# Row statistics ahead of the mixing stage, and a filter's wrap-around term added by accumulating DMAs, in a gated convolution and token-mixing kernel

## The chip, the cores and the metric

The kernel runs on one core of one Trainium2 chip. The metric is the device time of one execution in microseconds (us), the lower the better. The profile's "span" runs from the first to the last recorded instruction and is about 1.8 us shorter than the reported time (203.6 against 205.44 in the profiled run of the kernel before). All times given as positions ("at 50.2") count from the start of the span.

The engines are named as in the profile: PE is TensorE (matmul), DVE is VectorE, ACT is ScalarE, POOL is GpSimd. SP issues most DMAs. "Granted clock" is the share of TensorE's full clock that its throttle let through.

## The reference

For x = q of shape [2048, 640], in bf16:

```python
g = sigmoid((x * gate_w).sum(-1))            # one gate per row
# a: a short convolution of k (4 taps), times v, then a long causal convolution, times q
kv = short_conv(k, shift_k) * v
a  = q * (irfft(rfft(pad(kv, 4096)) * rfft(pad(ssm_k, 4096)))[:2048] + kv * ssm_D)
# b: LayerNorm over a row, then an MLP that mixes along the 2048 rows
h  = layernorm(x)                            # row mean and variance
u  = gelu(einsum("sd,sf->df", h, w1) + b1)   # F = 1536
b  = (einsum("df,fs->ds", u, w2) + b2).T
out = g * a + (1 - g) * b
```

The two halves a and b share only x, g and the last line. Matmuls of b can fill the time in which TensorE waits for data of a.

## The kernel before

The stages, with the names that the profile's tiles have:

- Filter spectra: TensorE turns `ssm` into `wT` and multiplies it with DFT matrices `FTB`; ScalarE copies the results from PSUM into `C[0]` and `C[1]`; VectorE's "mixing" finishes the spectra with additions and subtractions. The index h = 0 or 1 says which half of the 2048 positions is meant.
- kv: k is reordered (`kp<-kn`) and transposed by DMA into `KT`; 80 matmuls for each half (`KF,KT`) do the short convolution into `ksh`; VectorE multiplies with v (`vkv` for the first half, `kv` for the second).
- kv spectra: 64 matmuls per half (`vkv,FTB`, `kv,FTB`), evacuated by ScalarE into `C[2]` and `C[3]`, mixed by VectorE.
- MLP: 384 matmuls `X,ring` (first layer; X is x after normalising, `ring` holds the layer's weights as they are loaded), GELU into `GT`, 384 matmuls `GT,W` (second layer, with its weights `W`).
- Output: VectorE multiplies spectra (`tm<-C,C` and so on), TensorE transforms back with the matrices `GTB` (`C,GTB` and `SS,GTB`), VectorE multiplies by q and adds b.

While it is being built, the kernel puts all operations into a list scheduler, which has assumed durations, priorities (`prio`, the lower goes first) and the dependencies it finds from overlapping memory.

Memory is nearly full, so buffers share places. `GT`, the first layer's result, is 12 blocks of 1280 bytes per partition, and its place serves others earlier:

```python
        ksh = [alloc(f"ksh{i}", [128, 4, D], BF16, at=base_of(GT) + 5120 * (1 + i)) for i in range(2)]
        rows = alloc("rows", [20, 4, 512], BF16, at=base_of(GT))
        kp = [alloc("kp0", ..., at=base_of(ring[1]) + 10240), alloc("kp1", [128, NG, 128], BF16, at=base_of(GT))]
```

So the first four blocks of GT are also `kp1` (the reordered k of blocks 1 and 3), and the other eight are `ksh`. The filter loop, v1mix, the gate and the first layer:

```python
        for h in range(2):
            # ... transposes of the filter
            for p in PORD:
                fwd(srcW(h), h, p, C[h], p, 1.0 / 1024.0, "W")      # forward DFT and evacuation
            for kt in range(2):
                for p in range(4):
                    ln_tile(2 * h + kt, p)          # bn_stats, bn_aggr on VectorE
                ln_apply(2 * h + kt)                # rstd on GpSimd, X=(X-mean)*rstd on VectorE
            if h == 0:
                for g0 in (0, 10):
                    tt("POOL", KF[:, g0:g0 + 10, :, :], ...)         # taps times a mask, on GpSimd
                for hk in range(2):
                    k_turn(hk)
                mixing(C[0], SS, 0, fine=True)
            else:
                mixing(C[1], C[0], 0)
        # ...
        def v1mix(Wh, Ws, Vh, Vs):                  # V += or -= W, real and imaginary parts exchanged
            def ap(h, s, o, st):
                return V(h, s * SL + o, [[SL, 2], [st, 2], [1, D]])
            tt("DVE", ap(Vh, Vs, 0, 3 * D), ap(Vh, Vs, 0, 3 * D), ap(Wh, Ws, 2 * D, -D), ALU.add)
            tt("DVE", ap(Vh, Vs, D, D), ap(Vh, Vs, D, D), ap(Wh, Ws, 3 * D, -3 * D), ALU.subtract)

        v1mix(C[0], 2, C[1], 2)
        v1mix(SS, 0, C[0], 0)
        # ... kv and its spectra ...
        for ft in range(FT):
            vt = _VT("mlp")
            for hk in range(4):
                # 8 matmuls X,ring per hk; prio 10**6 + 4*ft + hk: they fill what is left
                mms(vt, items, prio=10 ** 6 + 4 * ft + hk, name="m1")
            act(GT[:, ft, :]..., two, ACT.Gelu_apprx_tanh, ..., vt=vt, prio=0, name="gelu")
        # ...
        tt("POOL", gth[:, :], vtmp[:, :], rstd[:, :], ALU.mult)      # the gate, 128x16 elements
        # ... seven more small operations, tanh on ScalarE among them
```

## Time and profile before

| | before |
|---|---|
| time, median of 3 runs | 205.58 us (205.1 to 205.8) |
| span of the profiled run, mean granted clock | 203.6 us, 0.975 |
| TensorE busy, VectorE busy | 180.8 us (89%), 182.0 us (89%) |

Five lines of the profile's page for the kernel before: the busy time of each engine, three rows of the view in 40 slices (each digit the busy share, or the granted clock, in tenths; a slice is 5.1 us), and the engines' shares of the chain of work that ended last.

```profile
PE 180.8 (89%) x1403; PEld 131.5 (65%) x1403; DVE 182.0 (89%) x193; ACT 116.1 (57%) x183; POOL 48.8 (24%) x33
...
PE   0769989951599999999999799999999999999993
...
DVE  8896999989989999989999999999949957997462
...
PEclk9999999996589999999999999999999999999999
...
PE 67%; DVE 17%; POOL 6%; DMA 3%; issue 2%; ACT 2%; SPq 0%; DVEq 0%; POOLq 0%
```

TensorE and VectorE are equally busy. From the ninth to the eleventh slice (41 to 56) TensorE falls to 5, 1 and 5 tenths, and its clock is low from the tenth to the twelfth. Where is the time lost? The timeline of TensorE has the answer. Its columns are the start, the duration, the engine, line, operation, output and inputs with shapes, the count, and in brackets the idle time before and what ended it.

```profile
39.06 4.33 PE L293 MATMUL pp<-KF,KT 128*128 128x128 bf16 x80
50.17 0.69 PE L293 MATMUL pp<-vkv,FTB 128*128 128x320 bf16 x2 [6.78 <-DVE vkv L617]
52.95 10.00 PE L293 MATMUL pp<-vkv,FTB 128*128 128x320 bf16 x54 [2.09 <-DVE vkv L617]
...
113.13 17.55 PE L293 MATMUL pp<-X,ring 128*128 128x320 bf16 x128 [1.46 <-ACT GT L655]
...
186.12 4.56 PE L293 MATMUL pp<-C,GTB 128*128 128x320 bf16 x32
...
194.91 5.60 PE L293 MATMUL pp<-GT,W 128*128 128x320 bf16 x40
```

After the short convolution (to 43.4) TensorE has nothing until 50.17, does two matmuls and waits again until 52.95; both waits end with VectorE's `vkv`. Then 54 matmuls take 10.00 us, 0.185 each, while later ones of the same shape take 0.136 to 0.137 (17.55/128). A smaller pause of 1.46 stands at 111.7. At the end 40 second-layer matmuls (5.60) come after the last inverse transform.

The same stretch by windows: length, then busy time and count of PE, PEld (weight loads), DVE, ACT and POOL, then the granted clock, the DMA share and GB/s.

```profile
43.40:50.10 6.70, 0.00 (x0) 0.00 (x0) 6.70 (x12) 1.39 (x2) 0.00 (x0) 0.80 0.94 391
50.10:52.90 2.80, 0.69 (x2) 0.14 (x2) 2.80 (x4) 0.00 (x0) 0.00 (x0) 0.50 0.38 78
```

VectorE is busy in all of this time, 6.70 of 6.70 us: it is not slow to start but has other work ahead of `vkv`. The mean clock is 0.80 in the first window and 0.50 in the second. The Trainium skill ("TensorE: Matmul & The Clock Gate", section "Part 1: The HAM clock gate") says that TensorE drops to half its clock after an idle window of about 3.4 us and regains it after a busy one; this trace agrees for the 6.78 us pause: in finer windows the granted clock is 1.00 up to 47.4, which is 4.0 us into the pause, then 0.50, and 1.00 again from 58.0.

VectorE's timeline in the kernel before, same columns:

```profile
48.54 1.48 DVE L617 TENSOR_TENSOR vkv<-ksh,vkv 128x2560 bf16<-128x2560 bf16 x1
...
51.41 1.48 DVE L617 TENSOR_TENSOR vkv<-ksh,vkv 128x2560 bf16<-128x2560 bf16 x1
...
64.11 2.88 DVE L617 TENSOR_TENSOR C<-C,C 128x2560 bf16<-128x2560 bf16 x2
66.91 2.88 DVE L617 TENSOR_TENSOR C<-C,SS 128x2560 bf16<-128x2560 bf16 x2
...
121.57 2.83 DVE L617 TENSOR_TENSOR tm<-C,C 128x5120 bf16<-128x5120 bf16 x1
...
181.52 2.89 DVE L617 TENSOR_TENSOR C<-SS 128x2560 bf16<-128x2560 bf16 x2
```

The two `vkv` products come at 48.54 and 51.41. The four additions of v1mix are the `C<-C,C x2` and `C<-C,SS x2` at 64.1 to 69.8, 5.6 us. The last two lines are landmarks: the first product of the output stage at 121.57, and the step at 181.52 whose first half (done at about 183.0) the last inverse half needs.

And GpSimd's two slowest gate operations:

```profile
74.20 14.03 POOL L627 TENSOR_SCALAR gpre<-mv,gws 128x16 f32<-128x16 f32 x1 [16.99 <-ACT junk L655]
105.53 5.67 POOL L617 TENSOR_TENSOR gth<-gth,gacc 128x16 f32<-128x16 f32 x1 [17.31 <-ACT junk L655]
```

They have 16 elements per partition and take 14.03 and 5.67 us (`gpre` and `gth` are intermediate values of the gate; `junk` is the discarded output of ScalarE's row sums). They do not compute for that long: the next addition of the same size took 0.77. From 74.20 to 88.02 VectorE went through eleven instructions with hardly a gap and then paused for 0.59; the first one ended in that pause.

### The profile page before, as it was taken

The page shows a single profiled execution, that of the slowest core. Times are in us where ns is not written, and L with a number is a line of the kernel's source. Part 1 is how long each engine was busy: PE and PEld are TensorE (multiplying, and loading weights), DVE is VectorE, ACT ScalarE, POOL GpSimd, SP SyncE. Part 2 cuts the span into 40 slices and gives each one's busy share as a digit, 9 for nine tenths or more (in the row PEclk, how much of TensorE's full clock was granted, in tenths as well). Part 3 has the DMA queues.
Part 4 walks back from the last instruction along what each step waited for, and adds up shares of the span by engine and source line. Part 5 has one row for each costly group of instructions (what it writes and reads, how often), then busy time and mean ns, then how long its engine had stood idle before and what let it go on. Part 6 is the DMA issues. An engine that isn't in the chain of part 4 may idle for free.

```text
span 203.6 us, 3356 instructions
## 1 busy us (share of the span) xinstructions
PE 180.8 (89%) x1403; PEld 131.5 (65%) x1403; DVE 182.0 (89%) x193; ACT 116.1 (57%) x183; POOL 48.8 (24%) x33
## 2 busy tenths in 40 slices
PE   0769989951599999999999799999999999999993
PEld 0446555640357877777776577788888867887672
DVE  8896999989989999989999999999949957997462
ACT  4798999970388989899640312123223164433752
POOL 2539700020520049930029600521000000000000
PEclk9999999996589999999999999999999999999999
DMA  5999999997898000007502700499999903110122
GB/s 165 338 405 278 344 335 197 198 400 322 159 229 283 5 0 0 0 3 234 178 3 63 246 0 3 106 236 315 236 306 404 351 11 129 69 64 0 64 93 104
DMA packets 35631, 35.00 MB, mean 172 GB/s; under 512 B 15515, under 2 KB 32544, under 8 KB 35616
## 3 DMA queue, kind: packets, MB, share of 16 engines
q1 hardware_dynamic: 34464, 32.15, 51.0%
q0 software_dynamic: 1088, 2.62, 6.8%
q8 instruction: 11, 0.18, 0.4%
q14 instruction: 4, 0.03, 0.0%
q10 hardware_dynamic: 64, 0.01, 0.0%
HBM read 25.87 MB, written 2.62 MB: 140 GB/s over the span
## 4 chain that ended last, share of the span: by engine, by line
PE 67%; DVE 17%; POOL 6%; DMA 3%; issue 2%; ACT 2%; SPq 0%; DVEq 0%; POOLq 0%
PE pp L293 67%; DVE X L628 4%; DVE stats L842 4%; DMA X<-in_A_q_dram 3%; DVE C L617 3%; POOL gth L617 3%; DVE SS L617 3%; POOL KF L617 2%; DVE kp L724 1%; DVE vkv L617 1%; POOL rstd L617 1%; ACT junk L655 1%; DVE mv L844 1%; SPq L267 0%; POOL gpre L617 0%
## 5 line engine op out<-in xcount | busy, mean ns | idle before, releaser
L293 PE MATMUL pp<-X,ring 128*128 128x320 bf16 x384 | 53.6, 299 | 1.5 <-ACT GT L655 1.5
L293 PE MATMUL pp<-GT,W 128*128 128x320 bf16 x384 | 52.9, 299 | 0.0
L617 DVE TENSOR_TENSOR C<-C 128x2560 bf16<-128x2560 bf16 (+1 forms) x28 | 48.7, 1766 | 3.2 <-DMA C<-C 2.6
L293 PEld LDWEIGHTS pp<-GT,W 128*128 128x128 bf16 x384 | 43.5, 114 | 8.8 <-ACT O L655 0.2
L293 PEld LDWEIGHTS pp<-X,ring 128*128 128x128 bf16 x384 | 37.4, 98 | 16.2 <-issue 1.8
L655 ACT ACTIVATE C<-pp 128x640 bf16<-128x640 f32 x64 | 40.0, 794 | 12.6 <-PE pp L293 12.1
L655 ACT ACTIVATE O<-pp,c,omg 128x640 bf16<-128x640 f32 (+1 forms) x17 | 14.5, 852 | 34.5 <-PE pp L293 34.5
L617 DVE TENSOR_TENSOR tm<-C,C 128x2560 bf16<-128x2560 bf16 (+1 forms) x12 | 22.7, 1926 | 0.0
L293 PE MATMUL pp<-wT,FTB 128*128 128x320 bf16 x128 | 20.1, 313 | 0.5 <-ACT wT L655 0.4
L655 ACT ACTIVATE GT<-pp,cc 128x640 bf16<-128x640 f32 x12 | 9.4, 789 | 18.6 <-PE pp L293 18.6
L293 PE MATMUL pp<-vkv,FTB 128*128 128x320 bf16 x64 | 11.9, 351 | 8.9 <-DVE vkv L617 8.9
L627 POOL TENSOR_SCALAR gpre<-mv,gws 128x16 f32<-128x16 f32 x1 | 14.0, 14028 | 17.0 <-ACT junk L655 17.0
L617 DVE TENSOR_TENSOR C<-tm 128x1280 bf16<-128x1280 bf16 (+1 forms) x16 | 17.9, 1153 | 0.2
L655 ACT ACTIVATE cgb<-pp,gg 128x640 bf16<-128x640 f32 x16 | 12.7, 793 | 8.0 <-PE pp L293 8.0
L293 PEld LDWEIGHTS pp<-wT,FTB 128*128 128x128 bf16 x128 | 10.8, 101 | 9.5 <-ACT C L655 4.4
L293 PEld LDWEIGHTS pp<-vkv,FTB 128*128 128x128 bf16 x64 | 6.6, 111 | 13.9 <-issue 6.9
L293 PE MATMUL pp<-ident,ssm 128*128 128x128 bf16 x80 | 8.8, 267 | 6.7 <-DMA ssm<-in_A_ssm_k_dram 5.4
L842 DVE BATCH_NORM_STATS2 stats<-X 128x6 f32<-128x320 bf16 x32 | 13.6, 463 | 0.5 <-DMA X<-in_A_q_dram 0.5
L293 PE MATMUL pp<-C,GTB 128*128 128x320 bf16 x96 | 13.7, 299 | 0.0
L628 DVE TENSOR_SCALAR X<-X,mv,rstd 128x640 bf16<-128x640 bf16 x16 | 9.6, 667 | 3.6 <-POOL rstd L617 3.6
L293 PEld LDWEIGHTS pp<-ident,ssm 128*128 128x128 bf16 x80 | 6.3, 128 | 9.2 <-DMA ssm<-in_A_ssm_k_dram 5.4
L655 ACT ACTIVATE junk<-gq 128x640 bf16<-128x640 bf16 x16 | 11.8, 736 | 0.5
(62 smaller groups left out, 195.2 us busy)
## 6 DMA issues: line engine op xcount, KB each, us to landing
ring<-in_B_w_dram SPq DMA_DIRECT2D x12, 512.0 KB, 6.0
W<-in_B_w_dram SPq DMA_DIRECT2D x8, 768.0 KB, 9.4
ssm<-in_A_ssm_k_dram SPq DMA_DIRECT2D x4, 640.0 KB, 9.0
X<-in_A_q_dram SPq DMA_DIRECT2D x4, 640.0 KB, 9.1
kn<-in_A_k_dram SPq DMA_DIRECT2D x4, 640.0 KB, 7.3
C<-C POOLq DMA_DIRECT2D x4, 640.0 KB, 11.7
out_dram<-O SPq DMA_DIRECT2D x7, 320.0 KB, 2.3
vkv<-in_A_v_dram SPq DMA_DIRECT2D x2, 640.0 KB, 5.2
```

The lines of the kernel that those rows point to most:

```text
L293: ins = self.nc.tensor.matmul(ps_ap, lhsT=lhsT, rhs=rhs, start=start, stop=stop, skip_group_check=True)
L617: return SC.add(eng, d, lambda s: T.op(eng, lambda e: e.tensor_tensor(o, a, b, op), [a, b], [o]), [a, b], [o], prio=prio, name="tt")
L627: return e.tensor_scalar(o, a, s1, None, op0=op0)
L628: return e.tensor_scalar(o, a, s1, s2, op0=op0, op1=op1)
L655: return T.op("ACT", lambda e: e.activation(o, src, func, **kw), rr + [src], ww)
L724: SC.add("DVE", 0.85, lambda s: T.op("DVE", lambda e: e.tensor_copy(ov, iv), [i[:, :, :]], [o[:, :, :]]), [i[:, :, :]], [o[:, :, :]], prio ...
L842: SC.add("DVE", 0.46, (lambda o, i: lambda s: T.op("DVE", lambda e: e.bn_stats(o, i), [i], [o]))(o, i), [i], [o])
L844: SC.add("DVE", 0.2, (lambda o, i: lambda s: T.op("DVE", lambda e: e.bn_aggr(o, i), [i], [o]))(o, i), [i], [o])
```

## The change

The intent: finish the row statistics and x early, so that first-layer matmuls can run while kv is not there; take 5.6 us of additions from VectorE, the co-bound engine, by letting DMAs accumulate; and free the gate chain from GpSimd. The accumulating DMAs used here add, so the signs must be in the stored spectra already: some ScalarE evacuations get a negative scale, mixing of the later half and the cross products get other signs, and GTB's imaginary part is negated on ScalarE ahead of the second inverse half. There is also a one-line move of `kp1`, from GT's place to GTB's.

```diff
-        kp = [alloc("kp0", ...), alloc("kp1", [128, NG, 128], BF16, at=base_of(GT))]
+        kp = [alloc("kp0", ...), alloc("kp1", [128, NG, 128], BF16, at=base_of(GTB))]
 ...
-            for kt in range(2):
-                for p in range(4):
-                    ln_tile(2 * h + kt, p)
-                ln_apply(2 * h + kt)
+                fwd(..., (lambda c, k2: k2 == 1) if h == 0 else (lambda c, k2: c == 1))   # negative scales
             if h == 0:
+                for hk in range(4):
+                    for p in range(4):
+                        ln_tile(hk, p)
+                    ln_apply(hk)
 ...
-                mixing(C[1], C[0], 0)
+                mixing(C[1], C[0], 0, conj=True)
 ...
         def v1mix(Wh, Ws, Vh, Vs):
-            tt("DVE", ap(Vh, Vs, 0, 3 * D), ap(Vh, Vs, 0, 3 * D), ap(Wh, Ws, 2 * D, -D), ALU.add)
-            tt("DVE", ap(Vh, Vs, D, D), ap(Vh, Vs, D, D), ap(Wh, Ws, 3 * D, -3 * D), ALU.subtract)
+            for i in range(2):
+                dma(V(Vh, (Vs + i) * SL, [[1280, 2], [1, 1280]]), V(Wh, (Ws + i) * SL + 1280, [[-1280, 2], [1, 1280]]),
+                    128 * 5120 * 2, stream="POOL", prio=0, accum=True)
 ...
-        tt("POOL", gth[:, :], vtmp[:, :], rstd[:, :], ALU.mult)      # and six more of the gate
+        tt("DVE", gth[:, :], vtmp[:, :], rstd[:, :], ALU.mult, mode=1, prio=0)
 ...
-                tt("DVE", comp(V1[g], i, 0), comp(T1, 0, 0), comp(T1, 0, 1), ALU.subtract)
-                tt("DVE", comp(V1[g], i, 1), comp(T1, 1, 0), comp(T1, 1, 1), ALU.add)
+                tt("DVE", comp(V1[g], i, 0), comp(T1, 0, 0), comp(T1, 0, 1), ALU.add)
+                tt("DVE", comp(V1[g], i, 1), comp(T1, 1, 1), comp(T1, 1, 0), ALU.subtract)
 ...
         inverse(1, Z1)
+        for p in (0, 2, 1, 3):
+            gk = GTB[:, p, :, :, 1, :]
+            act(gk, gk, ACT.Copy, scale=-1.0, name="neg")
```

More of the change, by code (lines that the diff above doesn't have):

```diff
@@ L592, in _build @@
         kn = [alloc(f"kn{i}", [128, 4, D], BF16, at=base_of(ring[1]) + 5120 * i) for i in range(2)]
-        kp = [alloc("kp0", [128, NG, 128], BF16, at=base_of(ring[1]) + 10240), alloc("kp1", [128, NG, 128], BF16, at=base_of(GT))]
+        kp = [alloc("kp0", [128, NG, 128], BF16, at=base_of(ring[1]) + 10240), alloc("kp1", [128, NG, 128], BF16, at=base_of(GTB))]
         pint = alloc("pint", [128, 4, 2, 2, 256], I32, at=base_of(ring[1]))
@@ L806, in transp, with fwd @@
             act(wT[:, hk, p, :], full, ACT.Copy, vt=vt, name="wT")
-        def fwd(src, h, p, dst, slot, scale, name):
+        def fwd(src, h, p, dst, slot, scale, name, neg=lambda c, k2: False):
             for k2 in range(2):
@@ L817, in fwd, with mixing @@
                     o = dst[:, slot, 2 * c + k2, :].rearrange("p (a b) -> p a b", a=2)
-                    kw = {} if scale is None else {"scale": scale}
+                    sc = -scale if neg(c, k2) else scale
+                    kw = {} if sc == 1.0 else {"scale": sc}
                     act(o, two, ACT.Copy, vt=vt, name=name + "e", **kw)
-        def mixing(R, Th, Ts, fine=False):
+        def mixing(R, Th, Ts, fine=False, conj=False):
             def sl(h, s, n=1):
@@ L833, in mixing @@
             oB = V(Th, Ts * SL, [[3 * 1280, 2], [1, 1280]])
+            if conj:
+                oA, oB = oB, oA
             tt("DVE", oA, pr(R, 0), pr(R, 1, True), ALU.add)
@@ L859, in _build @@
             for p in PORD:
-                fwd(srcW(h), h, p, C[h], p, 1.0 / 1024.0, "W")
-            for kt in range(2):
-                for p in range(4):
-                    ln_tile(2 * h + kt, p)
-                ln_apply(2 * h + kt)
+                fwd(srcW(h), h, p, C[h], p, 1.0 / 1024.0, "W", (lambda c, k2: k2 == 1) if h == 0 else (lambda c, k2: c == 1))
             if h == 0:
+                for hk in range(4):
+                    for p in range(4):
+                        ln_tile(hk, p)
+                    ln_apply(hk)
                 for g0 in (0, 10):
@@ L886, in v1mix @@
         def v1mix(Wh, Ws, Vh, Vs):
-            def ap(h, s, o, st):
-                return V(h, s * SL + o, [[SL, 2], [st, 2], [1, D]])
-            tt("DVE", ap(Vh, Vs, 0, 3 * D), ap(Vh, Vs, 0, 3 * D), ap(Wh, Ws, 2 * D, -D), ALU.add)
-            tt("DVE", ap(Vh, Vs, D, D), ap(Vh, Vs, D, D), ap(Wh, Ws, 3 * D, -3 * D), ALU.subtract)
+            for i in range(2):
+                dma(V(Vh, (Vs + i) * SL, [[1280, 2], [1, 1280]]), V(Wh, (Ws + i) * SL + 1280, [[-1280, 2], [1, 1280]]),
+                    128 * 5120 * 2, stream="POOL", prio=0, accum=True)
         v1mix(C[0], 2, C[1], 2)
@@ L922, in _build @@
         for p in PORD:
-            fwd(lambda kt, p, ci: vkv0[:, kt, p, 320 * ci:320 * ci + 320], 0, p, C[2], p, None, "A")
+            fwd(lambda kt, p, ci: vkv0[:, kt, p, 320 * ci:320 * ci + 320], 0, p, C[2], p, 1.0, "A")
         mixing(C[2], C[1], 0)
@@ L927, in _build @@
         for p in PORD:
-            fwd(lambda kt, p, ci: kv1[:, kt, p, 320 * ci:320 * ci + 320], 1, p, C[3], p, None, "A")
+            fwd(lambda kt, p, ci: kv1[:, kt, p, 320 * ci:320 * ci + 320], 1, p, C[3], p, 1.0, "A", lambda c, k2: k2 == 1)
         mixing(C[3], C[2], 0)
@@ L955, in _build @@
                         act(junk[:, :], gb[:, b, :], ACT.Copy, acc=gacc[:, t:t + 1], name="gsum")
-        tt("POOL", gth[:, :], vtmp[:, :], rstd[:, :], ALU.mult)
-        tt("POOL", gth[:, :], gth[:, :], gacc[:, :], ALU.mult)
-        ts("POOL", gpre[:, :], mv[:, :, 0], gws[:, 0:1], None, ALU.mult)
-        tt("POOL", gpre[:, :], gpre[:, :], gth[:, :], ALU.add)
-        act(gth[:, :], gpre[:, :], ACT.Tanh, scale=0.5)
-        ts("POOL", gg[:, :], gth[:, :], 0.5, 0.5, ALU.mult, ALU.add)
-        ts("POOL", omg[:, :], gth[:, :], -0.5, 0.5, ALU.mult, ALU.add)
-        tt("POOL", c2[:, :].rearrange("p (a b) -> p a b", a=4), omg[:, :].rearrange("p (a b) -> p a b", a=4), b2f, ALU.mult)
+        tt("DVE", gth[:, :], vtmp[:, :], rstd[:, :], ALU.mult, mode=1, prio=0)
+        tt("DVE", gth[:, :], gth[:, :], gacc[:, :], ALU.mult, mode=1, prio=0)
+        ts("DVE", gpre[:, :], mv[:, :, 0], gws[:, 0:1], None, ALU.mult, mode=1, prio=0)
+        tt("DVE", gpre[:, :], gpre[:, :], gth[:, :], ALU.add, mode=1, prio=0)
+        act(gth[:, :], gpre[:, :], ACT.Tanh, scale=0.5, prio=0)
+        ts("DVE", gg[:, :], gth[:, :], 0.5, 0.5, ALU.mult, ALU.add, mode=1, prio=0)
+        ts("DVE", omg[:, :], gth[:, :], -0.5, 0.5, ALU.mult, ALU.add, mode=1, prio=0)
+        tt("DVE", c2[:, :].rearrange("p (a b) -> p a b", a=4), omg[:, :].rearrange("p (a b) -> p a b", a=4), b2f, ALU.mult, mode=1, prio=0)
         def w2_load(hk):
```

## The prediction

> **What bounds it now.** Times are microseconds from the span's start (span 203.6; the reported time is about 2 longer). The page gives TensorE 89%, VectorE 89%; the chain of waits is 67% TensorE. TensorE has three losses (timeline, windows): a hole from 43.4 to 52.95 (only two matmuls), because kv reaches it late through VectorE's queue; a granted clock of 0.50 just after, so that 54 matmuls took 10.0 instead of 7.4 at the later pitch of 0.136; and a 1.5 hole at 111.7, where ScalarE sat 6.7 behind the gate chain on GpSimd. VectorE hardly idles before 146: a second, nearly equal bound.
>
> **What changes.** (1) All row statistics come before mixing, so x is normalised by about 40 instead of 58.4. The order view then puts 80 first-layer matmuls (10.9 at 0.136) ahead of the kv spectra, into the hole. (2) v1mix's four additions leave VectorE (5.6, at 64.1 to 69.7) for four accumulating DMAs. The existing four took 11.7 to land (median); the new ones are issued near 62 and needed from 87, so no wait. (3) The gate chain leaves GpSimd, where one 128x16 operation took 14.0 and one 5.7 while VectorE ran without a break. That agrees with the Trainium skill, "SBUF — State Buffer", section "SBUF: two separate sides": the port pair the two share is locked for a whole instruction. On VectorE it is eight operations of 0.1 to 0.2. (4) Four sign flips of GTB on ScalarE, estimated 0.6 each, are hidden.
>
> **Critical path, by hand in the new order with the trace's durations.** VectorE: normalising still loses 4 behind GpSimd's KF product (one instruction took 4.07 at 20.3); x blocks come at about 25, 28, 33 and 40, and TensorE waits about 2 to 4 for them. kv is ready at 55 to 56 (now 52.9). TensorE starts its spectra near 57 without having stopped and ends them near 70 (now 65), 104 first-layer matmuls further on. VectorE runs dry at about 64 and waits to 70 for these spectra: this swallows the 5.6 that v1mix freed. At the first inverse products (now 121.6) it stands at 121 to 125, the upper end because the tanh queues behind a GELU on ScalarE. TensorE, some 12 ahead, does 320 instead of 240 second-layer matmuls before the first inverse transform (near 163, as now) and has none left at the end. The last inverse half waits for VectorE: it starts near 184 (now 186.1), takes 8.7, then a tail of 4 to 4.5 (now 3.1, after 5.6 of second-layer work). Span about 197.
>
> **Prediction: 199.0 us, 194.0 to 203.5.** Faster by over 2%: 0.75; within 2%: 0.20; slower: 0.05. Much of TensorE's recovered 12 is not cashed, because VectorE becomes the bound.
>
> **Right if** the profile shows: no TensorE hole over 3 between 43 and 53, clock 1.0 there; VectorE busy about 177 instead of 182, with a new idle stretch of 4 to 7 near 64 to 70 ended by ScalarE's evacuation of kv spectra; the hole at 111.7 gone; TensorE waiting 1 to 6 for VectorE before the last inverse half; inverse matmuls last.
>
> **Wrong if** GpSimd's small column copy for the second half of k loses the race for the shared ports and waits for a VectorE pause (TensorE would stall several microseconds near 57); if the new DMAs land over 20 late and stop the cross products; or if the tanh holds VectorE longer than 2. Faster than 194 if the wait near 64 to 70 is much shorter.

## More of the kernel before

No engine has a fixed program order in the source.

```python
# in _Sched.add: an evacuation's dependencies are put on the first matmul of its group
            else:
                for d in deps:
                    if d.vt is not vt:
                        if d not in vt.first.deps:
                            vt.first.deps.add(d)
```

## The result

| | before | after |
|---|---|---|
| time, median of 4 runs | 205.69 us (205.1 to 205.93) | 198.8 us (197.93 to 199.71) |
| ratio of fast runs, 95% interval | | 0.967 (0.961 to 0.973) |
| span of the profiled run, granted clock | 203.6 us, 0.975 | 196.1 us, 0.996 |
| TensorE, VectorE busy | 180.8, 182.0 us | 177.4, 177.0 us |

Ratios here and below are the mean time of one kernel's fast runs over the mean time of the kernel before's fast runs in the same rounds on the same chip, so they are not quite the ratio of the medians quoted. Executions over 1.5% slower than the fastest of the same kernel are left out of the means. The kernel is faster by 3.3%.

The same five lines of the page, for the changed kernel (a slice is now 4.9 us):

```profile
PE 177.4 (90%) x1403; PEld 131.4 (67%) x1403; DVE 177.0 (90%) x196; ACT 118.5 (60%) x187; POOL 28.6 (15%) x30
...
PE   0759987999999999999999999999999979997890
...
DVE  7996998799999179999999879999999599989994
...
PEclk9999999999999999999999999999999999999998
...
PE 67%; DVE 16%; DMA 9%; ACT 3%; POOL 2%; issue 2%; SPq 0%; DVEq 0%
```

The low slices of TensorE and the dip of its clock are gone. VectorE has a new low slice, the fourteenth (64 to 69). The share of DMA in the chain rose from 3% to 9%, because the loads of k now stand in it (5%, by the page's list by line).

TensorE's timeline, after:

```profile
25.09 0.44 PE L293 MATMUL pp<-X,ring 128*128 128x320 bf16 x2 [0.32 <-DVE X L628]
...
31.49 1.42 PE L293 MATMUL pp<-X,ring 128*128 128x320 bf16 x8 [0.76 <-DVE X L628]
...
39.37 1.43 PE L293 MATMUL pp<-X,ring 128*128 128x320 bf16 x8 [0.49 <-DVE X L628]
...
46.06 4.33 PE L293 MATMUL pp<-KF,KT 128*128 128x128 bf16 x80
50.23 4.51 PE L293 MATMUL pp<-X,ring 128*128 128x320 bf16 x32
...
55.37 0.43 PE L293 MATMUL pp<-vkv,FTB 128*128 128x320 bf16 x2
...
182.28 4.63 PE L293 MATMUL pp<-C,GTB 128*128 128x320 bf16 x32 [2.22 <-DVE C L617]
186.80 4.51 PE L293 MATMUL pp<-SS,GTB 128*128 128x320 bf16 x32
```

First-layer matmuls (`X,ring`) now run from 23.8 on. Eighty of them precede the first `vkv,FTB` at 55.37, 32 of them from 50.23 on, in the old hole. Three short waits for x remain, 0.32, 0.76 and 0.49, and one of 2.22 before the last inverse half. Nothing but that half's 64 matmuls is left at the end.

VectorE's timeline, after:

```profile
20.33 4.35 DVE L724 COPY kp<-kn 128x2560 bf16<-128x2560 bf16 x1
...
53.14 2.89 DVE L617 TENSOR_TENSOR vkv<-ksh,vkv 128x2560 bf16<-128x2560 bf16 x2
55.94 8.68 DVE L617 TENSOR_TENSOR C<-C 128x5120 bf16<-128x5120 bf16 x5
69.90 2.83 DVE L617 TENSOR_TENSOR C<-C 128x5120 bf16<-128x5120 bf16 x1 [5.28 <-ACT C L655]
...
114.54 0.17 DVE L628 TENSOR_SCALAR gg<-gth 128x16 f32<-128x16 f32 x1 [1.14 <-ACT gth L655]
...
123.71 2.83 DVE L617 TENSOR_TENSOR tm<-C,C 128x5120 bf16<-128x5120 bf16 x1
...
180.74 2.89 DVE L617 TENSOR_TENSOR C<-SS 128x2560 bf16<-128x2560 bf16 x2
```

The copy `kp<-kn` at 20.33 took 4.35 us where its siblings took 0.8: GpSimd's product KF ran from 19.97 to 24.00. `vkv` is ready at 54.5 and 56.0, 3 to 4.5 us later than before, but TensorE no longer stands still for it. v1mix is gone from VectorE, and in its place stands a wait of 5.28 for ScalarE's evacuation of the kv spectra. The first product of the output stage starts at 123.71, 2.1 us later than before, and the landmark step at 180.74, only 0.8 earlier.

GpSimd's timeline, after: the issues of the four new DMAs.

```profile
60.60 2.64 POOL L262 DMA_DIRECT2D C<-C  x2 [21.72 <-DVE C L617]
64.92 2.43 POOL L262 DMA_DIRECT2D C<-SS  x2 [1.68 <-DVE C L617]
```

They landed after 11.3 and 13.0 us (medians of the two groups; the first also contains the four that were there before). The four new ones alone took between 7.7 and 14.5 us. They are needed from 86 on, and no wait names them.

### Where 7.5 us come from

The spans differ by 7.5 us. At the end of the program they can be added up. The last inverse half starts 3.8 us earlier (182.28 against 186.12). The 5.6 us of second-layer matmuls after it are gone, since they found room earlier. The tail from the last matmul to the end is 1.7 longer (196.1 − 191.3 = 4.8 against 203.6 − 200.5 = 3.1), and the half itself takes 0.2 longer. 3.8 + 5.6 − 1.7 − 0.2 = 7.5.

Seen from TensorE, about 13 us were recovered: the wait of 8.9, some 2.6 of slow clock (10.0 − 54 × 0.136), and 1.5. About 6.6 were not cashed: 1.6 of waits for x, 1.1 for an output evacuation, 2.2 for VectorE, and 1.7 of tail. The difference of 6.4 leaves about 1 of the 7.5 to small changes of TensorE's busy time.

### The profile page after: what moved, and what is told of

Its sections match the earlier page's. It is cut to its first block, busy times and chain, and to the rows that moved or that the text cites. A ratio compares the mean times of both kernels' runs of the same rounds, so it can differ in the third digit from the quotient of the medians.

```text
span 196.1 us, 3370 instructions
## 1 busy us (share of the span) xinstructions
PE 177.4 (90%) x1403; PEld 131.4 (67%) x1403; DVE 177.0 (90%) x196; ACT 118.5 (60%) x187; POOL 28.6 (15%) x30
## 4 chain that ended last, share of the span: by engine, by line
PE 67%; DVE 16%; DMA 9%; ACT 3%; POOL 2%; issue 2%; SPq 0%; DVEq 0%
PE pp L293 67%; DMA kn<-in_A_k_dram 5%; DMA X<-in_A_q_dram 4%; DVE kp L724 3%; DVE stats L845 2%; DVE C L617 2%; DVE SS L617 2%; DVE X L628 2%; ACT ksh L655 2%; DVE vkv L617 1%; DVE cgb L617 1%; DVE O L617 1%; POOL rstd L617 1%; POOL vtmp L627 1%; ACT cgb L655 1%
## 5 line engine op out<-in xcount | busy, mean ns | idle before, releaser
L293 PE MATMUL pp<-X,ring 128*128 128x320 bf16 x384 | 55.5, 299 | 1.6 <-DVE X L628 1.6
L293 PEld LDWEIGHTS pp<-X,ring 128*128 128x128 bf16 x384 | 36.6, 98 | 17.6 <-DVE X L628 2.0
L655 ACT ACTIVATE O<-pp,c,omg 128x640 bf16<-128x640 f32 (+1 forms) x17 | 14.5, 853 | 37.9 <-PE pp L293 37.9
L262 POOL DMA_DIRECT2D C<-C x6 | 7.5, 1406 | 90.1 <-DVE C L617 90.1
L655 ACT ACTIVATE GT<-pp,cc 128x640 bf16<-128x640 f32 x12 | 9.5, 792 | 14.6 <-PE pp L293 14.5
L293 PEld LDWEIGHTS pp<-wT,FTB 128*128 128x128 bf16 x128 | 11.9, 102 | 7.8 <-ACT C L655 2.3
L293 PEld LDWEIGHTS pp<-C,GTB 128*128 128x128 bf16 x96 | 9.2, 98 | 6.4 <-DVE C L617 2.5
L655 ACT ACTIVATE wT<-pp 128x640 bf16<-128x640 f32 x16 | 10.2, 711 | 2.6 <-PE pp L293 2.6
L655 ACT ACTIVATE ksh<-pp 128x1024 bf16<-128x1024 f32 (+1 forms) x12 | 9.6, 893 | 3.2 <-PE pp L293 3.2
## 6 DMA issues: line engine op xcount, KB each, us to landing
C<-C POOLq DMA_DIRECT2D x6, 640.0 KB, 11.3
```

What stands on the lines that cost most here:

```text
L262: ins = engobj.dma_start(out_ap, in_ap, accum_op=ALU.add, max_dma_last_dim=2560)
L293: ins = self.nc.tensor.matmul(ps_ap, lhsT=lhsT, rhs=rhs, start=start, stop=stop, skip_group_check=True)
L655: return T.op("ACT", lambda e: e.activation(o, src, func, **kw), rr + [src], ww)
```

## The experiments

The question is which part made the gain. Theory A: statistics first fill the hole, as the prediction said. Rival B: the DMAs in v1mix's place, which unburden VectorE. Rival C, found after the result: the move of `kp1`, which the prediction never mentioned, is what allows early first-layer groups. Twelve runs were made, one of them (e5) of the changed kernel again; all results were correct. "Before" in each list of edits means that the edit is made to the kernel before; "changed", to the changed one.

### e1: statistics first and the kp1 move; v1mix and the gate as before

```diff
 (before)
+ kp1 at base_of(GTB); ln_tile/ln_apply for all four hk inside "if h == 0", ahead of mixing(C[0])
```

> The kernel before, with the row statistics first and the buffer kp1 moved, v1mix on VectorE and the gate on GpSimd as before. If the gain comes from filling TensorE's hole (main theory): 199 to 202 us, no TensorE idle over 3 us near 43 to 53, VectorE busy near 182. If it comes from taking v1mix's 5.6 us off VectorE (rival): 204 to 206 us.

Measured: median 198.03 us of its three fast runs and one slow one (201.92), ratio 0.962 (0.958 to 0.967). That is the whole gain, without the DMAs, and the time lies a little below the 199 to 202 us expected of the main theory. What happened in the slow run (clock 0.985) no profile shows. VectorE's timeline shows why the DMAs were not needed:

```profile
56.32 8.67 DVE L617 TENSOR_TENSOR C<-C 128x5120 bf16<-128x5120 bf16 x5
64.91 2.88 DVE L617 TENSOR_TENSOR C<-C,C 128x2560 bf16<-128x2560 bf16 x2
67.72 2.88 DVE L617 TENSOR_TENSOR C<-C,SS 128x2560 bf16<-128x2560 bf16 x2
70.52 2.82 DVE L617 TENSOR_TENSOR C<-C 128x5120 bf16<-128x5120 bf16 x1
```

v1mix fills almost exactly the time in which VectorE of the changed kernel waits: here the first mixing step of the kv spectra starts at 70.52, there at 69.90. The pause of TensorE by the gate chain stays (1.19 us), and costs nothing that shows in the time.

### e2: v1mix by DMAs only

```diff
 (changed)
- statistics first, kp1 at base_of(GTB), gate on VectorE
+ statistics per half, kp1 at base_of(GT), gate on GpSimd
```

> The kernel before, with only the accumulating DMAs and the sign-adjusted spectra. Main theory: 203.5 to 206 us, the TensorE hole at 43 to 53 stays, and VectorE, with about 177 us of work, gets a new idle stretch. Rival (VectorE's work is what counts): 199 to 201 us.

Measured: 205.78 us, ratio 0.999 (0.994 to 1.003). The hole stays, with pauses of 6.49 and 2.09 before the kv spectra, as TensorE's timeline shows for the first:

```profile
50.32 0.69 PE L293 MATMUL pp<-vkv,FTB 128*128 128x320 bf16 x2 [6.49 <-DVE vkv L617]
```

VectorE waits 1.99 for the spectra in v1mix's place. Rival B falls as the cause: 5.6 us off a busy engine bought nothing.

### e3: only the kp1 move

```diff
 (before)
-        alloc("kp1", [128, NG, 128], BF16, at=base_of(GT))
+        alloc("kp1", [128, NG, 128], BF16, at=base_of(GTB))
```

> The kernel before, with only the buffer kp1 moved off the first layer's output tile. The prediction gave the early first-layer matmuls to the order of the row statistics; then this run stays at 204.5 to 206.5 us. Rival: the old place of kp1 is what forbade early first-layer matmuls; then most of the gain is here already, 200 to 203 us, with about 40 first-layer matmuls ahead of the kv spectra.

Measured: 200.38 us, ratio 0.973 (0.968 to 0.977). One line makes 5 of the 7 us. TensorE's timeline:

```profile
43.03 1.86 PE L293 MATMUL pp<-X,ring 128*128 128x320 bf16 x8 [2.24 <-DVE X L628]
...
54.06 1.25 PE L293 MATMUL pp<-vkv,FTB 128*128 128x320 bf16 x8
```

There are 48 first-layer matmuls before the kv spectra, which start at 54.06 after no pause to speak of. Since x is late here (statistics not first), TensorE waits 2.24 for it at 40.8. Against e1, of the same rounds, 2.3 us are missing, and the two intervals do not touch: that is what statistics first add on top.

### e4: the changed kernel with kp1 back in GT's place

```diff
 (changed)
-        alloc("kp1", [128, NG, 128], BF16, at=base_of(GTB))
+        alloc("kp1", [128, NG, 128], BF16, at=base_of(GT))
```

> The changed kernel with kp1 back on the first layer's output tile. If the order of the row statistics is what fills the hole, as the prediction put it: within 1 us of the changed kernel, 198 to 200 us. If the place of the buffer decides: the hole at 43 to 53 is back and the time is 203 to 206 us, although statistics, v1mix and gate are all as changed.

Measured: 206.83 us, ratio 1.005 (1.001 to 1.009). Everything else of the change is there, statistics first included, and the gain is gone; the time is even a little above the expected 203 to 206 us. TensorE's timeline:

```profile
50.55 0.69 PE L293 MATMUL pp<-vkv,FTB 128*128 128x320 bf16 x2 [7.37 <-DVE vkv L617]
56.07 8.04 PE L293 MATMUL pp<-vkv,FTB 128*128 128x320 bf16 x42 [4.83 <-DVE vkv L617]
```

The hole is back and longer, with no first-layer matmul in it. The scheduler's rule quoted above tells why: the first group of GELU results goes to `GT[:, 0]`, that place is `kp1` until the DMA has transposed the last block of k, and so the group's first matmul may not start. In e4 those transposes are issued at 51.17 and after, and the first `X,ring` matmuls run at 63.95. This reading of the rule is from the code; the runs show that the move of the buffer decides (e3 and e4, in both directions). The second `vkv` product even comes 3.1 us later than in the kernel before (54.53 against 51.41), behind more row work. Theory A as the prediction put it falls, and rival C stands, with A as its second part.

### e5: the changed kernel again, in the rounds of e6 to e8

> The changed kernel once more, for a comparison on one chip with the runs of this call: 197.5 to 200 us.

Measured: 199.48 us (198.01 to 199.6), ratio 0.967 (0.960 to 0.974). The changed kernel has two levels: about 198.0 at a mean clock of 0.994 to 0.996, and about 199.6 at 0.988 to 0.990. This profile caught the upper level. First TensorE's timeline, then the window from 184 to 186 (columns as before):

```profile
182.25 6.20 PE L293 MATMUL pp<-C,GTB 128*128 128x320 bf16 x32 [2.22 <-DVE C L617]
```

```profile
184.00:186.00 2.00, 2.00 (x9) 1.18 (x8) 2.00 (x2) 0.82 (x2) 0.00 (x0) 0.50 0.00 0
```

The pause of 2.22 us is the same as in the profile above, but here the clock drops to 0.50 afterwards, and 32 matmuls take 6.20 instead of 4.63: the 1.6 us between the two levels.

### e6: GpSimd's product KF in pieces, so that it blocks no normalising

```diff
 (changed)
-                for g0 in (0, 10):
-                    tt("POOL", KF[:, g0:g0 + 10, :, :], ..., ALU.mult)
+                kf(0, 10, [])
+                kf(10, 5, [X[:, 1, 3, 0:1]])    # also reads x: starts when block 1 is normalised
+                kf(15, 5, [X[:, 2, 3, 0:1]])
```

> The changed kernel, with the second half of GpSimd's KF product cut in two and made to wait for normalised blocks of x, so that it runs beside VectorE's statistics instead of its normalising and its copies of k. If GpSimd's product is what held the 4.35 us copy at 20.3 (port lock), that copy falls to 0.8 us, kv is ready 2 to 4 us earlier, TensorE's waits for x and for VectorE near 180 shrink, and the time is 195.5 to 197.5 us. If the copy was slow because of its data (landing of k), nothing changes: 198 to 200 us.

Measured: 195.96 us, ratio 0.953 (0.946 to 0.959). The medians of e5 and e6 are 3.5 us apart, but this overstates the gain, since e5's median lies on the upper level and e6's on the lower (e6: 195.90 to 195.98 us at a clock of 0.994 to 0.995, and 196.90 us at 0.989 in the profiled execution). Level against level it is 2.1 us (195.9 against 198.0) to 2.6 us (196.9 against 199.5). The copy that took 4.35 us:

```profile
21.09 0.82 DVE L724 COPY kp<-kn 128x2560 bf16<-128x2560 bf16 x1
```

The pieces of KF now take 2.58 and 2.07, each not far from half of the old 4.03, while VectorE's row statistics keep their pace (0.83 for two, as elsewhere). The kv spectra start at 53.24 instead of 55.37, and everything after is 2 to 3 us earlier. One part of the expectation failed: TensorE's pause before the last inverse half did not shrink, it is again 2.22, and in this profile the clock falls to 0.50 after it as in e5 (32 matmuls in 6.20). The Trainium skill ("SBUF — State Buffer", section "SBUF: two separate sides") says that VectorE and GpSimd share a port pair as an exclusive lock, held for a whole instruction. The 4.35 us in the changed kernel and the 0.82 us here agree with it.

### e7: another assumed rate for accumulating DMAs, which only reorders

```diff
 (changed)   # in acc_dma, the four that add the products; 320.0 is the default of the scheduler's model
-                dma(o, i_, 128 * 5120 * 2, stream="POOL", prio=0, accum=True)
+                dma(o, i_, 128 * 5120 * 2, stream="POOL", prio=0, accum=True, rate=110.0)
```

> The changed kernel, with the scheduler told that an accumulating DMA is slow (its assumed rate 110 in place of 320), which only reorders instructions. VectorE's 2.6 us wait for the accumulated spectra near 152 and TensorE's 2.2 us wait near 180 should go, and second-layer matmuls are last again: 195.5 to 198 us if VectorE's chain to the inverse transforms is the bound of the end, as the prediction says; 198 to 200 us if not.

Measured: 209.13 us, ratio 1.016 (1.010 to 1.023). This was a miss, a slowdown of 1 to 2%. The idea was to make the scheduler expect the DMAs as late as they land, and so to fill VectorE's wait of 2.57 at 151.7. But with the late estimate it put the whole chain for the last output half ahead of the first one, and TensorE stood still:

```profile
173.41 7.33 PE L293 MATMUL pp<-C,GTB 128*128 128x320 bf16 x32 [12.84 <-DVE C L617]
```

### e8: e6 and e7 together

```diff
 (changed)
+ the edits of e6 and e7
```

> Both of the two runs before together: 193.5 to 196.5 us if the two waits are independent. TensorE's own work, 177 us busy plus 5.3 us of waiting for the first load and 3 us of tail, forbids less than about 187 us.

Measured: 206.87 us, ratio 1.005 (0.998 to 1.013). A miss for the same cause: TensorE waits 12.8 before its first inverse transform, as in e7.

### e9: e6 with an assumed rate of 290

```diff
 (changed, with the edit of e6)
+                dma(o, i_, 128 * 5120 * 2, stream="POOL", prio=0, accum=True, rate=290.0)
```

> The run with the KF product split, with the assumed rate of the accumulating DMAs at 290 instead of 320: the order of TensorE is unchanged, and on VectorE the two products of the last inverse half now stand ahead of the addition that waits for the accumulated spectra. VectorE's 2.3 us wait near 150 should be filled, TensorE's 2.2 us pause before the last inverse half shrinks below 1, and its clock after it stays at 1.0: 192.5 to 195 us. If that pause is not set by VectorE's chain: 195.5 to 197 us, as without.

Measured: 194.00 us (194.0 to 194.05), ratio 0.944 (0.939 to 0.948). With this small step of the rate the scheduler puts the second product (`tm<-C,SS`) ahead of the addition that waits for the DMA. VectorE's timeline:

```profile
146.35 5.55 DVE L617 TENSOR_TENSOR tm<-C,SS 128x5120 bf16<-128x5120 bf16 x2
151.82 1.49 DVE L617 TENSOR_TENSOR C<-C 128x2560 bf16<-128x2560 bf16 x1
```

The wait before that addition (2.57 in the changed kernel, 2.30 in e6) is gone. TensorE's timeline:

```profile
178.36 4.63 PE L293 MATMUL pp<-C,GTB 128*128 128x320 bf16 x32 [0.81 <-DVE C L617]
```

Its last half starts at 178.36 after a pause of 0.81 only, and the clock stays at 1.00 to the last matmul. Of the 2.3 us of wait in e6, 1.3 arrive at the last inverse half (it started at 179.69 there), so VectorE's chain is what binds the end of the changed kernel. The medians of e6 and e9, which are of different rounds, differ by 2.0; the other 0.7 are not located. Together with e12 below, which takes the same time, this is the fastest version, faster than both kernels.

### e10, e11, e12: do the DMAs and the gate's move help once other limits are gone?

e10 is e1 with the edit of e6 (v1mix on VectorE, gate on GpSimd):

> Statistics first and kp1 moved, v1mix on VectorE and the gate on GpSimd as before, with the KF product split. If v1mix's DMAs and the gate add nothing (main theory): 194.5 to 197 us, within 1 us of the changed kernel with the same split. If they pay once VectorE is tighter: 198 us or more.

Measured: 195.48 us, ratio 0.954 (0.946 to 0.961).

e11 is the changed kernel with v1mix back on VectorE and the old signs (gate on VectorE):

> The changed kernel with v1mix back on VectorE and the old signs, all else as changed. If the freed 5.6 us are swallowed by VectorE's wait for the kv spectra (the prediction): 198 to 200.5 us and no idle stretch of VectorE near 64 to 70. If the DMAs bring their 5.6 us: 203 us or more.

Measured: 198.49 us, ratio 0.965 (0.959 to 0.971). VectorE's timeline has v1mix from 64.58 on, and the first mixing step of the kv spectra follows it with no wait in brackets:

```profile
70.18 2.82 DVE L617 TENSOR_TENSOR C<-C 128x5120 bf16<-128x5120 bf16 x1
```

This run also separates the two edits: it differs from the changed kernel in v1mix and its signs alone (0.965 against 0.967), and from e1 in the gate alone (0.965 against 0.962). Neither pair shows a gain, though the runs are of different rounds.

e12 is e10 with the rate of 290, five rounds:

> The run with statistics first, kp1 moved and the KF product split, v1mix on VectorE and the gate on GpSimd as before, now also with the assumed rate of the existing accumulating DMAs at 290. If v1mix's DMAs and the gate do not matter even then: 193.5 to 195 us, as the changed kernel with the same two edits (194.0). If they pay once the other waits are gone: 196 us or more.

Measured: 194.14 us (193.89 to 194.72), ratio 0.944 (0.940 to 0.949).

So there are three pairs that differ in v1mix and the gate together, at three different levels of time:

| | v1mix by DMA, gate on VectorE | v1mix on VectorE, gate on GpSimd |
|---|---|---|
| the change itself | 0.967 (0.961 to 0.973), 198.8 us | 0.962 (0.958 to 0.967), 198.03 us (e1) |
| with KF in pieces | 0.953 (0.946 to 0.959), 195.96 us (e6) | 0.954 (0.946 to 0.961), 195.48 us (e10) |
| with the order of e9 as well | 0.944 (0.939 to 0.948), 194.00 us (e9) | 0.944 (0.940 to 0.949), 194.14 us (e12) |

All three pairs overlap. In the first and the third pair a gain of over about 1% from the two together is excluded (0.961/0.967 and 0.939/0.949 at the widest); a smaller one is left open. The two runs of a row are of different rounds, so read along a row only with the intervals in mind. In the first row the two levels matter too: on its lower level the changed kernel takes 198.0 us, as e1 does.

## Why the prediction was right or wrong

The number was right: 199.0 predicted, 198.8 measured, in the range of 194.0 to 203.5, and "faster by over 2%" held. Every point of its "Right if" list came true as well; none of them tests what lets the first-layer matmuls start early. Point by point:

- What binds it now: right. The hole from 43.4 to 52.95 and the slow clock after it are gone, and with them the time.
- Step (1), "All row statistics come before mixing ... The order view then puts 80 first-layer matmuls ... into the hole": the 80 matmuls came, but the cause named is not the one that lets them. Without the kp1 move the statistics bring nothing (e4, 206.83); the move alone brings 5 us (e3); the statistics add 2.3 (e1 against e3). The prediction read the outcome off the order of the changed kernel and gave it to the most visible edit of the diff. It did not mention the one-line edit at all. The sum was right because the order contained both; for the cause that it named, this is luck and no evidence.
- Step (2), v1mix: right that nothing waits for the DMAs, and right that the 5.6 us freed are swallowed by a wait for the kv spectra: predicted 4 to 7 near 64 to 70, measured 5.28 at 64.6 to 69.9. e1 and e11 confirm it by putting v1mix back, at no cost that could be measured.
- Step (3), the gate: the hole at 111.7 is gone, as predicted, and the tanh held VectorE for 1.14 ahead of `gg`. The operations on VectorE took 0.17 to 0.23; they are seven, not eight, since the tanh stays on ScalarE. On its own the move is worth nothing that could be measured (e11 against e1, which keeps GpSimd's gate and a pause of 1.19). The likely reason is that TensorE is later held by VectorE anyway (1.57 before e1's last half).
- Step (4), the sign flips: 0.62 each on ScalarE, hidden.
- Terms of the sum: waits for x 1.6 (2 to 4 predicted); kv ready at 54.5 to 56.0 (55 to 56); spectra from 55.4 to 69.0 (57 to 70); first inverse product at 123.7 (121 to 125); last half from 182.3 (184), taking 9.0 (8.7); tail 4.8 (4 to 4.5). The errors are small and lie on both sides; together they make the predicted span of 197 against 196.1.
- "Much of TensorE's recovered 12 is not cashed, because VectorE becomes the bound": right. VectorE's landmark step moved by 0.8 us only (181.52 to 180.74), and e9 shows that time saved on VectorE does arrive, if in part (1.3 of 2.3 us at the last half).
- None of the named risks came true: GpSimd's column copy ran in 0.28 at 38.60. One thing was not foreseen, the two levels of the changed kernel. In the one profile that there is of each level, the pause is 2.22 us in both, and a drop of the clock follows it only on the upper level.

What stays open: what the DMAs and the gate's move are worth separately below 1%, and why the same pause of 2.22 us drops the clock in some executions and not in others.

## What to carry to other kernels

Where a list scheduler and shared buffers decide the order, look at the allocations in a diff first: the place of one buffer can hold back a whole stage, and a reordering of code can stay without effect until that place is free. Work taken off an engine counts only if that engine is not about to wait for something else at that point; ask which wait ends last there. And before crediting a gain to the largest edit, run each edit alone and the whole change without it.

## What the Trainium skill lacked or had wrong

- "TensorE: Matmul & The Clock Gate", section "HAM oscillation — how this bites in real kernels", gives the rule that no idle gap of TensorE should exceed about 3.4 us. Here shorter pauses were followed by a clock of 0.50: a pause of 2.22 us at 180.0 in e5 (32 matmuls took 6.20 instead of 4.63), though not after the same pause in the first profile of the same kernel; one of 2.22 us in e6; and one of 2.24 us in e3 (clock 0.50 from 44.0 to 47.0). Pauses of 0.81 (e9) and 1.57 us (e1) at the same place left the clock at 1.00, and one of 2.99 (e11) was followed by 6.20 again. The page calls its window free-running, which may be why the same pause counts only sometimes; no run here shows it.
- "SBUF — State Buffer", section "SBUF: two separate sides", says that the loser of the shared port pair is blocked for a whole instruction of the other. A GpSimd operation on 128x16 elements got no turn between VectorE's back-to-back instructions either: it took 14.03 us over eleven of them and ended in VectorE's next pause of 0.59. The page does not tell that a waiting GpSimd can be passed over many times, which is how this trace reads. It isn't always so: from 111.28 on, operations of the same size took 0.41 to 1.43 us beside a busy VectorE.
- "DMA: Bandwidth & Descriptors", section "Anatomy of one DMA — SWDGE (gpsimd) path", has a fit per DMA of 2.0 us plus bytes over 436e3, from which an estimate for these of 655,360 bytes would be 3.5 us. No page has a figure for accumulating ones between places in SBUF: here the eight of the changed kernel landed after 7.7 to 15.3 us (median 11.7). They were issued in pairs, and of the new ones up to four were in flight at once, beside other transfers.
